# A Hyena-style block with a gated MLP on one core: queueing the first vector steps of each convolution behind the stage ahead, and moving the norm's small steps

## The chip, the core and the metric

The kernel runs on one core of a Trainium2 chip. The core has engines with a queue of instructions each: TensorE (PE) for matrix products, VectorE (DVE) and ScalarE (ACT) for elementwise work, GpSimd (POOL), and SyncE (SP), which issues the transfers here. [...]The time is that of one execution on the device in microseconds (us); before the change it is 519.38 us, the median of three runs (519.25 to 520.62). Inputs and weights are bf16.

## The reference, cut to what matters

There are 2048 rows of 576 values. A first half mixes along the rows (a shift convolution of four taps, a gate, a long convolution with a filter as long as the sequence), a second half is a gated MLP with 4608 hidden values. Both sit behind a layer norm with scales from a condition vector.

```python
h  = layernorm(x) * (1 + ca) + sa
# long convolution over the rows, written with FFTs in the reference
kv = shift4(k, shift_k) * v
y  = causal_conv(kv, ssm_k) + kv * ssm_D
x  = x + ga * (h * y)
h  = layernorm(x) * (1 + cb) + sb
x  = x + gb * ((silu(h @ w1) * (h @ w3)) @ w2)
```

## The kernel before

The rows are cut into 8 blocks of 256 (numbered `s`), two to a row block of 512 (`r` = 0 to 3). The long convolution is done block by block: the spectrum `X` of a block of `kv` and the spectrum `V` of a block of the filter (from two neighbouring pieces `W`) come from small matmuls with a Fourier basis; VectorE multiplies pairs of them and adds the products into `z`; small matmuls turn `z` back (`inverse`). The MLP of row block `r` runs on TensorE (`stream`: up and gate, then `down`), and while it runs the convolution of the two blocks of row block `r+1` is done beside it. That convolution is a Python generator: each `yield` says how many microseconds of VectorE work were recorded, and the MLP loop takes steps from it at a set rate (`advance`). The order in which the steps are recorded isn't yet that in the queues: a scheduler places each engine's instructions when the program is built, and puts a later recorded one ahead if it takes it to be ready and the engine to be free. `behind(engine)` keeps what is recorded under it behind the last instruction recorded for that engine so far.

```python
def behind(self, engine):
    last = [i for i in self.nc.cur_bb.bb.instructions if i.engine == engine.engine][-1]
    return self.tc.issue_after(last)

def kv_rows(self, s):                      # shift convolution and gate, 8 VectorE steps
    nc.vector.tensor_mul(kv[:], kh[:, 3:5, :], tap(0))
    yield 0.75
    for j in (1, 2, 3):
        nc.vector.tensor_mul(tmp[:], kh[:, 3 - j:5 - j, :], tap(j))
        nc.vector.tensor_add(kv[:], kv[:], tmp[:])
        yield 1.5
    nc.vector.tensor_mul(kv[:], kv[:], vt[:])
    ...

def v_block(self, s):                      # V from W(s) and W(s-1), 4 VectorE steps
    ...
        nc.vector.tensor_add(V[:, 0:6:3, :], W[:, 0:4:2, :], Wp[:, 1:4:2, :])
        nc.vector.tensor_sub(V[:, 1:6:3, :], W[:, 1:4:2, :], Wp[:, 0:4:2, :])
    ...

def pair(self, X, V, s, last=False):       # z(s) gets X * V
    if s not in self.accs:
        self.accs[s] = self.acc.tile([P, 6, D], BF16, name=f"z{s % 2}", tag=f"z{s % 2}")
        nc.vector.tensor_mul(self.accs[s][:], X[:], V[:])
        yield 2.0
        return
    p = self.prod.tile([P, 6, D], BF16, name="p", tag="p")
    with self.behind(nc.vector) if last else nullcontext():
        nc.vector.tensor_mul(p[:], X[:], V[:])
    yield 2.0
    nc.vector.tensor_add(z[:], z[:], p[:])
    yield 2.0

def conv(self, s0):                        # the two blocks s0, s1 of the next row block
    def filters():
        yield from self.k_rows(s1)
        yield -4.0
        yield from self.v_block(s0)
        yield from self.w_spectrum(s1)
    def old():
        V, X = self.old_v(s0 - 1, s0), self.old_x(1, s0)
        yield from self.pair(X, V, s0)
        for j in range(2, s0):
            ...                            # pairs of earlier blocks, for s1 and s0
        yield from self.gate_stats(s0)
        yield from self.kv_rows(s0)
        self.gate_var(s0)
    yield from self.mix(filters(), old())
    ...
    yield from self.mix(self.x_spectrum(s0), beside())   # TensorE reads kv(s0) here
    yield from self.x_sums(s0)
    yield from self.pair(self.X[s0], V0, s0)
    ...                                    # outcome(s0): inverse, residual, second norm;
                                           # kv_rows(s1), x_spectrum(s1) beside it; outcome(s1)

def hide(k):                               # MLP: one pair of tiles out of PSUM
    nc.scalar.activation(h3, gus[k][:, 0, :], ACT.Silu)
    nc.scalar.copy(u[:], gus[k][:, 1, :])
    nc.vector.tensor_mul(h3, h3, u[:])
    self.advance(rate * 2.05)              # steps of the convolution are recorded here
```

The row statistics go over three engines: ScalarE sums (`ln_sums`), VectorE and then GpSimd make `1/sqrt(var)` (`ln_var`), VectorE makes the shift (`ln_shift`), ScalarE applies both (`gate_rows` for the first norm, `normed_act` for the second).

Of the kernel before, what the change touches and what calls it, by code (L numbers as in the profile page):

```python
# [44 lines left out]
class _Kernel:  # L45
# [275 lines left out]
        nc.vector.tensor_add(both, both, odd)  # L321
        yield 1.5

    def kv_rows(self, s):

        nc = self.nc
        kh, vt = self.kh, self.vt
        kv = self.kvp.tile([P, 2, D], BF16, name="kv", tag="kv")
        tmp = self.kvp.tile([P, 2, D], BF16, name="kvt", tag="kvt")

        def tap(j):
            a = self.shk[:, j, :]
            return bass.AP(tensor=a.tensor, offset=a.offset, ap=[list(a.ap[0]), [0, 2], [1, D]])
        nc.vector.tensor_mul(kv[:], kh[:, 3:5, :], tap(0))
        yield 0.75
        for j in (1, 2, 3):
            nc.vector.tensor_mul(tmp[:], kh[:, 3 - j:5 - j, :], tap(j))  # L337
            nc.vector.tensor_add(kv[:], kv[:], tmp[:])  # L338
            yield 1.5
        nc.vector.tensor_mul(kv[:], kv[:], vt[:])  # L340
        self.kv = kv
        yield 0.75
# [38 lines left out]
            odd = self.kvp.tile([P, 2, D], BF16, name="Wo", tag="Wo")  # L381
            yield from self.forward2(self.Fk, self.kT, W[:, 0:2, :], odd[:], W[:, 2:4, :])

    def v_block(self, s):

        nc = self.nc
        W = self.Wl[s]
        V = self.spec.tile([P, 6, D], BF16, name="V", tag="V")
        if s == 0:
            nc.vector.tensor_copy(V[:, 0:6:3, :], W[:, 0:4:2, :])  # L390
            VS = W[:, 1:4:2, :]
        else:
            Wp = self.Wl[s - 1]
            nc.vector.tensor_add(V[:, 0:6:3, :], W[:, 0:4:2, :], Wp[:, 1:4:2, :])
            nc.vector.tensor_sub(V[:, 1:6:3, :], W[:, 1:4:2, :], Wp[:, 0:4:2, :])
            VS = V[:, 1:6:3, :]
        nc.vector.tensor_add(V[:, 2:6:3, :], V[:, 0:6:3, :], VS)
        yield 2.25
        nc.vector.tensor_sub(V[:, 1:6:3, :], VS, V[:, 0:6:3, :])
        self.V[s] = V  # L400
        yield 0.75

    def pair(self, X, V, s, last=False):

        nc = self.nc
        if s not in self.accs:
            self.accs[s] = self.acc.tile([P, 6, D], BF16, name=f"z{s % 2}", tag=f"z{s % 2}")
            nc.vector.tensor_mul(self.accs[s][:], X[:], V[:])  # L408
            yield 2.0
            return  # L410
        z = self.accs[s]
        p = self.prod.tile([P, 6, D], BF16, name="p", tag="p")
        with self.behind(nc.vector) if last else nullcontext():
            nc.vector.tensor_mul(p[:], X[:], V[:])  # L414
        yield 2.0
        nc.vector.tensor_add(z[:], z[:], p[:])  # L416
        yield 2.0
# [58 lines left out]
    def center(self, dst, src, mean, rstd):  # L476
        self.nc.vector.tensor_scalar(dst, src, mean, rstd, op0=ALU.subtract, op1=ALU.mult)

    def behind(self, engine):

        last = [i for i in self.nc.cur_bb.bb.instructions if i.engine == engine.engine][-1]
        return self.tc.issue_after(last)
# [10 lines left out]
    def gate_var(self, s):  # L493
        self.l1[s] = self.ln_var(*self.l1[s])

    def gate_rows(self, s):

        x1 = self.xo[s]
        r, b = self.ln_shift(*self.l1.pop(s))
        hg = self.lnp.tile([P, 2, D], BF16, name="hg", tag="hg")  # L500
        with self.behind(self.nc.scalar):
            for i in range(2):
                self.nc.scalar.activation(hg[:, i, :], x1[:, i, :], ACT.Identity, bias=b[:, i:i + 1],
                                          scale=r[:, i:i + 1])
        self.hg[s] = hg
# [56 lines left out]
        self.center(row[:, cc, 0:D], x1[:, cc, :], m, r)  # L562
        self.center(row[:, cc, D:640], x1[:, cc, 512:D], m, r)

    def normed_act(self, s, r, b):
        row, x1 = self.h2row, self.xo[s]
        for cc in range(2):
            for lo, hi, at in ((0, D, 0), (512, D, D)):
                self.nc.scalar.activation(row[:, cc, at:at + hi - lo], x1[:, cc, lo:hi], ACT.Identity,  # L569
                                          bias=b[:, cc:cc + 1], scale=r[:, cc:cc + 1])  # L570
# [168 lines left out]
    def outcome(self, s, fill, waits, between=None, quick=False):  # L739


        def steps():
            nc = self.nc
            yield self.real_parts(s)
            yield -waits[0]
            y = self.lnp.tile([P, 2, D], BF16, name="y", tag="y")
            for cc in range(2):
                nc.scalar.copy(y[:, cc, :].rearrange("p (h d) -> p h d", h=2), self.inverse(s, cc)[:, :, 0:H])
            yield -waits[1]
            self.residual(s, y)  # L750
            yield 1.5
            if between is not None:
                between()
            if quick:
                st = []
                for cc in range(2):
                    st.append(self.quick_stats(self.xo[s][:, cc, :], "l2"))
                    yield 1.25
                for cc in range(2):
                    self.normed(s, cc, *st[cc])  # L760
                    yield 0.75
            else:
                sums = [self.small.tile([P, 2], F32, name="l2" + k, tag=t) for k, t in (("s", "ssum"), ("q", "ssq"))]
                for i in range(2):
                    with self.behind(nc.scalar):
                        self.ln_sums(self.xo[s], i, *sums)
                    yield 0.0
                yield -waits[2] / 2
                stats = self.ln_var(*sums, "l2")
                yield -waits[2] / 2  # L770
                r, b = self.ln_shift(*stats)
                with self.behind(nc.scalar):
                    self.normed_act(s, r, b)
            yield -waits[3]
            self.accs.pop(s)
            self.hg.pop(s)
        yield from self.mix(steps(), fill)

    def turn_all(self, s):
# [6 lines left out]
    def conv_second(self):  # L786
        yield from self.gate_stats(1)
        yield from self.kv_rows(1)
        block = self.v_block(1)
        with self.behind(self.nc.vector):  # L790
            cost = next(block)
        yield cost

        def beside():
            yield from block
            self.gate_var(1)
            yield from self.pair(self.X[0], self.V[1], 1)
        yield from self.mix(self.x_spectrum(1), beside())
        self.mod_piece(5)
        self.gate_rows(1)  # L800
        yield from self.gate(1)
        self.load_k(2)
        yield from self.x_sums(1)
        yield from self.pair(self.X[1], self.V[0], 1)
        yield from self.outcome(1, self.mix(self.filter_ahead(2)), (5.0, 3.5, 0.0, 2.0), quick=True)
        self.turn_all(1)
        yield 0.0

    def conv(self, s0):
        s1 = s0 + 1  # L810
# [6 lines left out]
        def filters():  # L817
            yield from self.k_rows(s1)
            yield -4.0
            yield from self.v_block(s0)  # L820
            yield from self.w_spectrum(s1)

        def old():
            V, X = self.old_v(s0 - 1, s0), self.old_x(1, s0)
            yield from self.pair(X, V, s0)
            for j in range(2, s0):
                X = self.old_x(j, s0)
                yield from self.pair(X, V, s1)
                V = self.old_v(s0 - j, s0)
                yield from self.pair(X, V, s0)  # L830
            self.V1 = V
            yield from self.gate_stats(s0)
            yield from self.kv_rows(s0)
            self.gate_var(s0)
            if s0 == 2:
                yield from self.pair(self.X[0], self.V[s0], s0)
        yield from self.mix(filters(), old())
        X0, V0 = self.old_x(0, s0), self.old_v(0, s0)

        def beside():  # L840
            yield from self.v_block(s1)
            with self.behind(self.nc.sync):
                self.load_kv(s1)
            yield from self.gate_stats(s1)
            if s0 > 2:
                yield from self.pair(X0, self.V[s0], s0)
            self.X1 = self.old_x(1, s0)
            yield from self.pair(X0, self.V[s1], s1)
            self.gate_var(s1)
            self.gate_rows(s0)  # L850
            yield from self.gate(s0)
        yield from self.mix(self.x_spectrum(s0), beside())
        yield from self.x_sums(s0)
# [2 lines left out]
        def more():  # L856
            yield from self.pair(self.X1, self.V[s0], s1, True)
            yield from self.pair(self.X[s0], self.V1, s1)

        def others():  # L860
            yield from self.kv_rows(s1)
            yield from self.mix(self.x_spectrum(s1), more())
            yield from self.x_sums(s1)
        yield from self.outcome(s0, others(), (5.0, 4.5, 6.0, 0.0), lambda: self.gate_rows(s1))
# [317 lines left out]
```

## Time and profile before

| from the page of the profile | |
|---|---|
| span of the profiled execution | 516.6 us |
| PE busy | 495.2 us (96%) |
| DVE busy | 344.5 us (67%), 557 instructions |
| ACT busy | 293.6 us (57%) |
| POOL busy | 31.3 us (6%) |
| DMA | 107.80 MB, 209 GB/s |
| PEclk, all 40 slices | 9 tenths or more |

The page has the busy time of each engine, the span in 40 slices, and the chain of work that ended last. It calls a line of the kernel "L956" and an instruction by what it writes and reads. A matmul's end is modelled, so a busy PE isn't PE at its peak. By the first and last matmuls of lines 934, 945, 1046 and 1001, the MLP of r = 0 runs from about 34.5 us to 169.5 us, that of r = 1 to 290.6 us, that of r = 2 to 407 us, and that of r = 3 to the end. In r = 3 no convolution is left to do.

### The profile page before, as it was taken

Reading aid. Unit: us, or ns where it says so; the run is one execution under the profiler, and the core shown is the slowest. Engines: PE = TensorE matmul, PEld = TensorE weight load, DVE = VectorE, ACT = ScalarE, POOL = GpSimd, SP = SyncE. Lnnn points to the kernel's source line nnn. Section 1 sums busy time; section 2 is a strip of 40 time slices with the busy share of each in tenths; the row PEclk is TensorE's granted clock in tenths of the full one; section 3 lists DMA queues with packets and bytes.
Section 4 is the critical chain, followed back from the end, with each engine's and each line's share of the span. In section 5 each row is a group of like instructions: output and inputs, shape, how many; then the busy total and the mean of one; then the engine's idle time right before and its main releaser. Section 6 shows DMA issues by size and latency. Waiting matters only on the chain.

```text
span 516.6 us, 9251 instructions
## 1 busy us (share of the span) xinstructions
PE 495.2 (96%) x3650; PEld 293.5 (57%) x3650; DVE 344.5 (67%) x557; ACT 293.6 (57%) x581; POOL 31.3 (6%) x75
## 2 busy tenths in 40 slices
PE   7899899989899999999998999999999999999997
PEld 3567665456688444344676643444578644444775
DVE  8888899999997354979999626988972222222012
ACT  7658589657543468769443464886815355555000
POOL 3100000002000000000101000020000000000000
PEclk9999999999999999999999999999999999999999
DMA  8957949686979866558997559854555545532462
GB/s 271 301 173 217 313 157 299 194 256 212 293 236 355 264 211 196 177 164 275 333 318 203 161 151 349 315 201 124 174 139 140 159 123 164 173 111 76 117 182 69
DMA packets 102207, 107.80 MB, mean 209 GB/s; under 512 B 5075, under 2 KB 94228, under 8 KB 102164
## 3 DMA queue, kind: packets, MB, share of 16 engines
q1 hardware_dynamic: 102142, 107.21, 67.3%
q8 instruction: 28, 0.46, 0.4%
q14 instruction: 15, 0.12, 0.1%
q10 hardware_dynamic: 22, 0.01, 0.0%
HBM read 96.00 MB, written 11.21 MB: 208 GB/s over the span
## 4 chain that ended last, share of the span: by engine, by line
PE 66%; DVE 21%; ACT 5%; DMA 3%; issue 3%; POOL 2%; SPq 0%; DVEq 0%; POOLq 0%; ACTq 0%
PE ps L934 24%; PE ps L1046 21%; PE ps L1001 12%; DVE p L414 4%; PE ps L945 4%; DVE z L416 3%; DVE z L408 2%; DVE h L956 2%; DMA kh<-in_A_k_dram 2%; PE ps L316 2%; POOL l2r L454 1%; DVE kv L338 1%; DVE kvt L337 1%; ACT junk L446 1%; DMA wst<-in_B_w_dram 1%
## 5 line engine op out<-in xcount | busy, mean ns | idle before, releaser
L934 PE MATMUL ps<-h2T,wst 128*128 128x512 bf16 (+1 forms) x1056 | 200.6, 341 | 1.1 <-ACT W L318 0.8
L934 PEld LDWEIGHTS <-wst 128*128 128x128 bf16 x1056 | 100.2, 98 | 85.7 <-issue 13.8
L1046 PE MATMUL ps<-wst,h 128*128 128x288 bf16 x1152 | 145.0, 286 | 3.9 <-ACT u L955 2.0
L1046 PEld LDWEIGHTS <-h 128*128 128x128 bf16 x1152 | 112.2, 98 | 33.3 <-issue 4.8
L953 ACT ACTIVATE h<-ps 128x512 bf16<-128x512 f32 x108 | 64.8, 600 | 67.6 <-PE ps L945 42.1
L1001 PE MATMUL ps<-h2T,wst 64*128 64x512 bf16 x648 | 70.3, 377 | 0.2 <-DMA wst<-in_B_w_dram 0.2
L956 DVE TENSOR_TENSOR h<-h,u 128x512 bf16<-128x512 bf16 x108 | 45.0, 421 | 36.3 <-ACT u L955 36.2
L955 ACT CAST u<-ps 128x512 bf16<-128x512 f32 x108 | 63.4, 587 | 0.0
L414 DVE TENSOR_TENSOR p<-X,V 128x3456 bf16<-128x3456 bf16 x28 | 54.7, 1954 | 4.2 <-DMA V<-Vd 2.2
L416 DVE TENSOR_TENSOR z<-z,p 128x3456 bf16<-128x3456 bf16 x28 | 54.7, 1954 | 0.2
L1001 PEld LDWEIGHTS <-wst 64*128 64x128 bf16 x648 | 31.5, 94 | 38.7 <-DMA wst<-in_B_w_dram 0.7
L1016 DVE TENSOR_TENSOR h<-h,u 128x512 bf16<-128x512 bf16 x36 | 15.3, 426 | 55.3 <-ACT u L1015 55.3
L1013 ACT ACTIVATE h<-ps 128x512 bf16<-128x512 f32 x36 | 21.5, 598 | 36.5 <-PE ps L1001 36.5
L1063 DVE TENSOR_TENSOR og<-ps,gbrow 128x288 bf16<-128x288 f32 x32 | 13.2, 451 | 41.1 <-PE ps L1046 41.1
L446 ACT ACTIVATE junk<-x 128x576 bf16<-128x576 bf16 x54 | 37.2, 689 | 0.5
L945 PE MATMUL ps<-h2T,wst 64*128 64x512 bf16 (+1 forms) x264 | 33.0, 342 | 0.0
L604 ACT ACTIVATE h2T<-ps,sbcol,cbcol 128x256 bf16<-128x256 bf16 x35 | 16.7, 569 | 19.4 <-PE ps L574 19.4
L569 ACT ACTIVATE h2row<-x,l2n,l2r 128x576 bf16<-128x576 bf16 (+1 forms) x24 | 13.7, 643 | 19.4 <-DVE l2n L460 19.4
L454 POOL TENSOR_TENSOR l2r<-l2v,neghalf 128x2 f32<-128x2 f32 x6 | 11.2, 1868 | 181.2 <-DVE l2v L453 181.2
L337 DVE TENSOR_TENSOR kvt<-kh,shk 128x1152 bf16<-128x1152 bf16 x24 | 18.1, 754 | 4.3 <-DMA kh<-in_A_k_dram 4.2
L1015 ACT CAST u<-ps 128x512 bf16<-128x512 f32 x36 | 20.9, 581 | 0.0
L945 PEld LDWEIGHTS <-wst 64*128 64x128 bf16 x264 | 8.5, 94 | 21.0 <-issue 20.8
(140 smaller groups left out, 398.6 us busy)
## 6 DMA issues: line engine op xcount, KB each, us to landing
wst<-in_B_w_dram SPq DMA_DIRECT2D x80, 512.0 KB, 5.0
wst<-in_B_w_dram SPq DMA_DIRECT2D x72, 288.0 KB, 3.4
X<-Xd SPq DMA_DIRECT2D x8, 864.0 KB, 6.7
Xd<-X SPq DMA_DIRECT2D x6, 864.0 KB, 6.0
wst<-in_B_w_dram SPq DMA_DIRECT2D x80, 64.0 KB, 3.3
kh<-in_A_k_dram SPq DMA_DIRECT2D x7, 720.0 KB, 7.3
Vd<-V SPq DMA_DIRECT2D x4, 864.0 KB
V<-Vd SPq DMA_DIRECT2D x4, 864.0 KB, 9.6
```

Of the source, the lines that this page charges most:

```text
L337: nc.vector.tensor_mul(tmp[:], kh[:, 3 - j:5 - j, :], tap(j))
L414: nc.vector.tensor_mul(p[:], X[:], V[:])
L416: nc.vector.tensor_add(z[:], z[:], p[:])
L446: self.nc.scalar.activation(junk[:], src[:, i, :], func, scale=scale, accum_out=out[:, col:col + 1])
L934: nc.tensor.matmul(gus[k][:, i, a * n:(a + 1) * n], w[:, 5 * i + ct, (fi + a) * P:(fi + a + 1) * P], hT[:, ct, t0:t1], start=(first and ct ...
L945: nc.tensor.matmul(gus[k][:, i, a * n:(a + 1) * n], w[rows, 4, (fi + a) * P:(fi + a + 1) * P], hT[rows, 4, t0:t1], start=(first and a == 0 ...
L953: nc.scalar.activation(h3, gus[k][:, 0, :].rearrange("p (a t) -> p a t", a=m), ACT.Silu)
L955: nc.scalar.copy(u[:], gus[k][:, 1, :])
L956: nc.vector.tensor_mul(h3, h3, u[:].rearrange("p (a t) -> p a t", a=m))
L1001: nc.tensor.matmul(gus[f][:, i, :], w[rows, 5 * i + ct if ct < 4 else 4, cols], hT[rows, ct, :], start=swap == 0 and ct == 0, stop=swap == ...
L1013: nc.scalar.activation(h3, gus[f][:, 0, :], ACT.Silu)
L1046: nc.tensor.matmul(acc[t], self.h3[:, f0 + f, t * P:(t + 1) * P], w[:, f, :], start=(f0 + f == 0), stop=(f0 + f == NF - 1))
```

## The change

The convolution's first VectorE steps are to stay behind the stage ahead of them, so that the scheduler can't put them between steps that the stage ahead still waits for. The first product of a `z`, the first step and the three tap products of `kv_rows(s0)`, and the first two steps of `v_block(s0)` are now recorded under `behind(nc.vector)`. Apart from that, the last small step of each norm (`ln_shift`) gets a place of its own: `gate_shift` is recorded some steps after `gate_var` and ahead of `gate_rows`, and in the second norm a gap is left between `ln_shift` and the rows, which are recorded one row group at a time.

```diff
-    def kv_rows(self, s):
+    def kv_rows(self, s, last=False):
...
-        nc.vector.tensor_mul(kv[:], kh[:, 3:5, :], tap(0))
+        with self.placed(last):
+            nc.vector.tensor_mul(kv[:], kh[:, 3:5, :], tap(0))
         yield 0.75
         for j in (1, 2, 3):
-            nc.vector.tensor_mul(tmp[:], kh[:, 3 - j:5 - j, :], tap(j))
+            with self.placed(last):
+                nc.vector.tensor_mul(tmp[:], kh[:, 3 - j:5 - j, :], tap(j))
...
-    def v_block(self, s):
+    def v_block(self, s, last=False):
...
+            with self.placed(last):
+                nc.vector.tensor_add(V[:, 0:6:3, :], W[:, 0:4:2, :], Wp[:, 1:4:2, :])
+                nc.vector.tensor_sub(V[:, 1:6:3, :], W[:, 1:4:2, :], Wp[:, 0:4:2, :])
...                                            # pair: both first products
+            with self.placed(last):
+                nc.vector.tensor_mul(self.accs[s][:], X[:], V[:])
...
+    def placed(self, last):
+        return self.behind(self.nc.vector) if last else nullcontext()
...
+    def gate_shift(self, s):
+        self.l1[s] = self.ln_shift(*self.l1[s])
...
-        r, b = self.ln_shift(*self.l1.pop(s))
+        r, b = self.l1.pop(s)
...                                            # second norm
-                r, b = self.ln_shift(*stats)
-                with self.behind(nc.scalar):
-                    self.normed_act(s, r, b)
+                scales = self.ln_shift(*stats)
+                yield -3.0
+                for cc in range(2):
+                    self.normed_act(s, cc, *scales)
+                    yield -1.0
...                                            # conv
-            yield from self.v_block(s0)
+            yield from self.v_block(s0, True)
...
-            yield from self.pair(X, V, s0)
+            yield from self.pair(X, V, s0, True)
...
-            yield from self.kv_rows(s0)
+            yield from self.kv_rows(s0, True)
...
         def beside():
             yield from self.v_block(s1)
+            self.gate_shift(s0)
...
+            self.gate_rows(s0)
             yield from self.pair(X0, self.V[s1], s1)
             self.gate_var(s1)
-            self.gate_rows(s0)
...
         def others():
             yield from self.kv_rows(s1)
+            self.gate_shift(s1)
```

More of the change, by code (lines that the diff above doesn't have):

```diff
@@ L393, in v_block @@
             Wp = self.Wl[s - 1]
-            nc.vector.tensor_add(V[:, 0:6:3, :], W[:, 0:4:2, :], Wp[:, 1:4:2, :])
-            nc.vector.tensor_sub(V[:, 1:6:3, :], W[:, 1:4:2, :], Wp[:, 0:4:2, :])
+            with self.placed(last):
+                nc.vector.tensor_add(V[:, 0:6:3, :], W[:, 0:4:2, :], Wp[:, 1:4:2, :])
+                nc.vector.tensor_sub(V[:, 1:6:3, :], W[:, 1:4:2, :], Wp[:, 0:4:2, :])
             VS = V[:, 1:6:3, :]
@@ L407, in pair @@
             self.accs[s] = self.acc.tile([P, 6, D], BF16, name=f"z{s % 2}", tag=f"z{s % 2}")
-            nc.vector.tensor_mul(self.accs[s][:], X[:], V[:])
+            with self.placed(last):
+                nc.vector.tensor_mul(self.accs[s][:], X[:], V[:])
             yield 2.0
@@ L412, in pair @@
         p = self.prod.tile([P, 6, D], BF16, name="p", tag="p")
-        with self.behind(nc.vector) if last else nullcontext():
+        with self.placed(last):
             nc.vector.tensor_mul(p[:], X[:], V[:])
@@ L563, in normed, with normed_act @@
         self.center(row[:, cc, D:640], x1[:, cc, 512:D], m, r)
-    def normed_act(self, s, r, b):
+    def normed_act(self, s, cc, r, b):
         row, x1 = self.h2row, self.xo[s]
-        for cc in range(2):
+        with self.behind(self.nc.scalar):
             for lo, hi, at in ((0, D, 0), (512, D, D)):
@@ L788, in conv_second @@
         yield from self.kv_rows(1)
[L789 to L792, printed above, removed]
+        block = self.v_block(1, True)
+        yield next(block)
         def beside():
@@ L797, in beside @@
             yield from self.pair(self.X[0], self.V[1], 1)
+            self.gate_shift(1)
         yield from self.mix(self.x_spectrum(1), beside())
```

## The prediction

> **What bounds the kernel now.** I read the slices first, then TensorE's waits, then the timelines of PE and DVE around the longest waits. The slices say that PE hardly pauses.
>
> ```profile
> PE   7899899989899999999998999999999999999997
> DVE  8888899999997354979999626988972222222012
> PEclk9999999999999999999999999999999999999999
> ```
>
> PE is busy 495.2 of 516.6 us. Listing its pauses over 0.25 us in the timeline gives 14.6 us in all, so nothing that only removes waits can bring 3%. DVE is full from about 60 to 145 us (first half of r = 0's MLP and beyond), less so in r = 1 and 2. The longest pauses that this change could touch:
>
> ```profile
> PE ps L542 <- DVE z L528: 2.6, 1, 2.6
> PE ps L1046 <- ACT u L955: 2.0, 2, 1.5
> PE ps L542 <- DVE z L524: 1.9, 1, 1.9
> PE ps L1046 <- DVE og L1063: 1.9, 1, 1.9
> PE ps L367 <- ACT u L955: 0.9, 1, 0.9
> ```
>
> The third of them is what the change aims at. In the DVE timeline the next stage's first product (L408) stands between two steps of the inverse that TensorE waits for:
>
> ```profile
> 54.41 0.75 DVE L522 TENSOR_TENSOR z<-z 128x1152 bf16<-128x1152 bf16 x1
> 55.07 1.95 DVE L408 TENSOR_TENSOR z<-X,V 128x3456 bf16<-128x3456 bf16 x1
> 56.94 0.75 DVE L524 TENSOR_TENSOR z<-z 128x1152 bf16<-128x1152 bf16 x1
> ```
>
> But running ahead also fills holes. From 65.88 us DVE does `kv` for block 2 in time it had free; PE reads that `kv` (L316) much later:
>
> ```profile
> 65.88 0.76 DVE L334 TENSOR_TENSOR kv<-kh,shk 128x1152 bf16<-128x1152 bf16 x1
> 67.21 0.42 DVE L956 TENSOR_TENSOR h<-h,u 128x512 bf16<-128x512 bf16 x1
> 67.55 0.75 DVE L338 TENSOR_TENSOR kv<-kv,kvt 128x1152 bf16<-128x1152 bf16 x1
> 70.14 0.75 DVE L320 TENSOR_TENSOR W<-W,Wo 128x1152 bf16<-128x1152 bf16 x1
> 70.81 0.75 DVE L337 TENSOR_TENSOR kvt<-kh,shk 128x1152 bf16<-128x1152 bf16 x1
> 74.49 0.75 DVE L340 TENSOR_TENSOR kv<-kv,vt 128x1152 bf16<-128x1152 bf16 x1
> ```
>
> ```profile
> 79.39 0.41 PE L316 MATMUL ps<-kv,Fb 128*128 128x288 bf16 x2 [0.39 <-ACT u L955]
> ```
>
> In the next two row blocks the lead is larger. `kv` of block 4 is finished at 160.2 us and read first at 199.89; that of block 6 is read first at 331.40. So the stretches 146 to 170 us and 262 to 290 us, when PE works on `down`, carry the next block's convolution:
>
> ```profile
> 146.00:170.00 24.00, 24.00 (x208) 19.23 (x206) 18.17 (x26) 10.05 (x22) 0.69 (x1) 1.00 0.90 292
> 173.00:204.00 31.00, 31.00 (x157) 12.73 (x156) 15.02 (x29) 21.84 (x44) 0.69 (x1) 1.00 0.71 221
> 294.00:331.00 37.00, 37.00 (x185) 14.94 (x185) 21.37 (x28) 23.99 (x47) 0.00 (x0) 1.00 0.79 270
> ```
>
> (Columns: length; busy PE, PE loads, DVE, ACT, POOL; clock; DMA.) DVE is busy 18.2 of 24 us in the first, and only half of the time in the other two.
>
> [...]the granted clock is 1.00 throughout; this matters below.
>
> **The change part by part.** No instruction is added or removed: 559 on DVE before and after. It is order alone, so I set the order of each engine's instructions in the two built programs side by side and walked DVE's new order with durations from the old trace. Start to start in a full queue: 1.87 us for a 3456-wide step (55.07 to 56.94), 0.67 for a 1152-wide one (70.14 to 70.81), 0.34 for L956 (67.21 to 67.55).
>
> *r = 0.* L408 leaves the inverse of block 1, so PE's 1.87 us pause goes, and all up to the norm rows comes 1.87 earlier. Then DVE has nothing allowed but four L956 and two W steps; the last of these L956 waits for a tile that ACT released at 72.64, now 70.8, so L408 starts at about 71.2. From there to the end of `kv` the new order has 3 wide steps (5.6), 14 of 1152 (9.4), 2 L956 (0.7) and small ones (0.2): 15.9 us, so `kv` is ready at about 87.1 instead of 75.2. The W copies on ACT wait for V's second step, now 75.1 (74.6 before); PE resumes there at about 76.6, as before, which eats the 1.87. The scheduler moved only 16 matmuls ahead of L316, so PE asks at about 81.0 and waits **6.1 us**. From then on it is 6.0 behind the old trace. The inverse of block 2 still waits about 2 us for L528 (the shift taps of block 3 now also wait for `kh`, 7.3 us from issue to landing), and `kv` of block 3 costs perhaps 0.9. At the start of `down`, L367 now stands 48 matmuls into it, so its 1.55 us pause should go. Sum: 5.9 + 0.9 - 1.55 = **+5.3**.
>
> *r = 1.* Nearly nothing of blocks 4 and 5 stands in `down` any more. The convolution starts after r = 1's first L956, which ended 4.4 us after its first matmul (173.9 against 169.5). To the end of `kv` for block 4: 10 wide steps (18.7), 18 of 1152 (12.1), 13 L956 (4.4), small ones (0.2): 35.4 us, ready 39.8 us after the start. PE asks after 140 MLP matmuls in both programs, 199.89 - 169.52 = 30.4 us after the start. Wait **9.4 us**. Saved: the 0.93 at L367 (48 matmuls later now), 0.43 at L529 and 1.87 at `og`, since DVE is free when `og` comes. Sum: 9.4 - 3.2 = **+6.2**.
>
> *r = 2.* Start to first L956 3.8 us; then 16 wide steps (29.9), 18 of 1152 (12.1), 19 L956 (6.5), small ones (0.2): 48.7, ready at 52.5 us. PE asks at 331.40 - 290.63 = 40.8, plus 8 matmuls moved ahead (1.6): 42.4. Wait **10.1**, less 0.48 at the start of `down`: **+9.6**.
>
> *The norm's small steps.* `l1n` and `l2n` no longer hold DVE while POOL works (5.2 and 4.1 us of DVE idle time in all, 0.6 to 0.9 each). In r = 0, where DVE is full, this is worth about 1.6 us and is in the walk; elsewhere it lies beside other work.
>
> Together +21.1 us: 519.4 + 21.1 = 540.5. To that comes the clock. [...]I count less than half of it, since nothing here has shown it. Prediction: **542 us**.
>
> **The rivals.** (a) *The aim is met*: the waits for L524, L528, `og` and u go and nothing comes back, 519.4 - 1.9 - 2.6 - 1.9 - 2.5 = 510.5 us. For it speaks that these waits are really in the trace and that L408 really stands in the way. Against it, the half-idle stretches above: in r = 1 `kv` has a lead of 40 us today because it is done in `down`, and the new order forbids that. (b) *A wash*: the lost lead is absorbed because DVE is half idle from 173 to 204 us. That idle time is about 16 us, and in r = 0 some of the displacement is made up; if my sums were 10% too high the waits in r = 1 and 2 would shrink by 3.5 and 5, and with the gains the total would be near 531. To come to zero they would have to be 25% too high. (c) *Worse*: [...]Loads of old X and V wait for DVE to free a buffer, and weight loads stand behind them; with DVE 10 us late PE may wait for `wst` as well, and the clock may drop each time. That would give 550 to 556.
>
> **Range and chances.** The walk's durations are measured and PE's need for `kv` is a data dependence, so I hold slower to be nearly certain; the size hangs on 16 and 10 wide steps being counted right and on the clock. Range 527 to 556, low end from (b), high end from (c). Faster by over 2% 0.03, within 2% 0.12, slower by over 2% 0.85.
>
> **What would show it.** Among PE's waits a new group "L316 <- DVE kv" of three long ones, 6, 9 and 10 us; DVE nearly idle late in each `down`; `og`, L524 and L367 gone from the waits; PEclk under 9 in the slices of the long waits if the clock drops. I am wrong if no L316 waits over 3 us, or if DVE runs the convolution's steps faster than in the old trace.

## The result and the profile after

The changed kernel takes **548.15 us** (median; 547.61 to 548.30) against 519.58 us for the kernel before (519.25 to 520.62) beside it. The ratio is 1.054, with a 95% interval of 1.053 to 1.056: 28.6 us slower. The span of the profiled execution went from 516.6 to 546.2 us.

The slices first, the same three rows as before:

```profile
PE   7999986989999992999999999479999999999997
DVE  8889688898451898597832599979973121222011
PEclk9999987999999996999999999979999999999999
```

PE now has three holes (slices 7, 16, and 26 to 27), and behind each the granted clock falls under nine tenths. DVE's row shows the other side: slices 11 to 13 were nine, nine and seven and are now four, five and one, and at the holes it has seven to nine.

PE's waits name the holes (us in total, times, longest; two waits ahead of r = 0, of 3.0 and 1.0 us, are left out):

```profile
PE ps L316 <- DVE kv L342: 26.4, 4, 10.6
PE ps L947 <- ACT W L318: 1.9, 1, 1.9
PE ps L1059 <- ACT u L968: 0.9, 1, 0.9
```

L316, which reads `kv`, waited for nothing of note before. The waits for the inverse's `z` (2.6 and 1.9 us) and for `og` (1.9) are gone. In the timeline of PE the waits for `kv` are 5.14 us in r = 0, 9.79 in r = 1 and 10.60 in r = 2, and a small one of 0.85. Leaving out the wait ahead of the first matmul, PE's pauses over 0.1 us are 35.1 us, where they were 14.5. (The prediction's 14.6 us hold these, and not only those over 0.25 us, which are 13.3 us before and 33.7 after.)

The first aim is met. In DVE's timeline the inverse's steps stand together, with no product between them:

```profile
54.57 0.75 DVE L532 TENSOR_TENSOR z<-z 128x1152 bf16<-128x1152 bf16 x1
55.35 0.76 DVE L534 TENSOR_TENSOR z<-z 128x1152 bf16<-128x1152 bf16 x1
```

But that product (now L412) and all that is placed behind it come later, `kv` last:

```profile
71.43 1.95 DVE L412 TENSOR_TENSOR z<-X,V 128x3456 bf16<-128x3456 bf16 x1
73.30 0.75 DVE L335 TENSOR_TENSOR kv<-kh,shk 128x1152 bf16<-128x1152 bf16 x1
...
86.66 0.75 DVE L342 TENSOR_TENSOR kv<-kv,vt 128x1152 bf16<-128x1152 bf16 x1
```

```profile
87.55 1.12 PE L316 MATMUL ps<-kv,Fb 128*128 128x288 bf16 x4 [5.14 <-DVE kv L342]
```

Before, that last step began at 74.49 us, so `kv` is 12.2 us later and PE is waiting for it. The stretches that answer to the three of before (the first two at the same distance from the end of r = 0's `down`, the third 0.9 us nearer to the end of r = 1's):

```profile
153.00:177.00 24.00, 24.00 (x206) 19.19 (x205) 7.08 (x21) 10.69 (x23) 0.69 (x1) 1.00 0.93 301
180.00:211.00 31.00, 26.83 (x132) 10.81 (x133) 30.93 (x38) 19.79 (x39) 2.02 (x1) 0.98 0.69 212
308.00:345.00 37.00, 36.75 (x188) 15.34 (x192) 36.02 (x37) 24.03 (x48) 0.00 (x0) 1.00 0.88 308
```

In `down` DVE's busy time (the third figure after the length) fell from 18.2 to 7.1 us; in the next two row blocks it rose from 15.0 to 30.9 and from 21.4 to 36.0 us. Half-idle DVE time in r = 1 and 2 was filled, and it was not enough.

Two losses make up the span: PE's pauses, +20.6 us, and PE's busy time, 495.2 to 503.3 us, **+8.1 us** for the same work (the remaining 0.9 us is smaller gaps). The windows around the waits show where the second comes from (the column after POOL is the granted clock):

```profile
73.10:76.50 3.40, 0.89 (x8) 0.48 (x6) 3.40 (x8) 3.40 (x10) 0.17 (x1) 0.99 0.94 264
76.50:79.90 3.40, 3.40 (x16) 2.15 (x15) 3.40 (x4) 1.51 (x3) 1.04 (x1) 0.51 0.32 94
...
86.70:93.50 6.80, 5.73 (x17) 1.98 (x19) 6.41 (x10) 1.99 (x4) 0.00 (x0) 0.50 0.89 285
...
209.60:219.80 10.20, 3.02 (x9) 1.18 (x10) 7.12 (x10) 0.64 (x1) 4.30 (x1) 0.50 0.32 101
...
352.90:363.20 10.30, 4.36 (x12) 1.61 (x12) 9.62 (x12) 2.63 (x6) 2.72 (x1) 0.50 0.53 183
```

PE is busy for 3.40 + 5.73 + 3.02 + 4.36 = 16.5 us at half clock. From 76.49 us, at clock 0.51, 16 products of L947 (128x256) took 3.53 us; from 80.49, at full clock, 16 took 1.92. Half of the 16.5 us, 8.3 us, is an estimate of what PE would have saved at full clock; 8.1 us is the measured rise.

By the ends of the four `down` stages (last matmul), the row blocks' lengths:

| us | r = 0 | r = 1 | r = 2 | r = 3 |
|---|---|---|---|---|
| before | 169.7 | 121.1 | 116.2 | 105.8 |
| after | 176.8 | 129.0 | 130.5 | 106.2 |
| difference | +7.1 | +7.8 | +14.3 | +0.4 |

### The profile page after: what moved, and what is told of

Its sections match the earlier page's. It is cut to its first block, busy times and chain, and to the rows that moved or that the text cites. A ratio compares the mean times of both kernels' runs of the same rounds, so it can differ in the third digit from the quotient of the medians.

```text
span 546.2 us, 9253 instructions
## 1 busy us (share of the span) xinstructions
PE 503.3 (92%) x3630; PEld 295.8 (54%) x3650; DVE 344.5 (63%) x557; ACT 294.5 (54%) x581; POOL 29.6 (5%) x75
## 4 chain that ended last, share of the span: by engine, by line
PE 55%; DVE 29%; ACT 7%; DMA 4%; issue 2%; POOL 2%; SPq 0%; POOLq 0%; ACTq 0%; DVEq 0%
PE ps L1059 22%; PE ps L947 14%; PE ps L1014 12%; DVE z L420 6%; DVE p L418 6%; DMA wst<-in_B_w_dram 3%; DVE h L969 3%; PE ps L958 2%; ACT junk L450 2%; POOL l1r L458 2%; PE ps L316 2%; DVE z L412 1%; DVE kvt L339 1%; DVE kv L340 1%; PE ps L552 1%
## 5 line engine op out<-in xcount | busy, mean ns | idle before, releaser
L947 PE MATMUL ps<-h2T,wst 128*128 128x512 bf16 (+1 forms) x1037 | 205.2, 347 | 3.5 <-ACT W L318 1.9
L947 PEld LDWEIGHTS <-wst 128*128 128x128 bf16 x1056 | 102.2, 100 | 91.7 <-issue 21.4
L1014 PE MATMUL ps<-h2T,wst 64*128 64x512 bf16 x648 | 70.5, 376 | 0.4 <-DMA wst<-in_B_w_dram 0.4
L968 ACT CAST u<-ps 128x512 bf16<-128x512 f32 x108 | 63.2, 585 | 0.0
L969 DVE TENSOR_TENSOR h<-h,u 128x512 bf16<-128x512 bf16 x108 | 45.2, 421 | 18.8 <-ACT u L968 18.7
L1014 PEld LDWEIGHTS <-wst 64*128 64x128 bf16 x648 | 31.2, 94 | 39.4 <-DMA wst<-in_B_w_dram 1.7
L316 PE MATMUL ps<-kv,Fb 128*128 128x288 bf16 x48 | 10.4, 318 | 26.4 <-DVE kv L342 26.4
L318 ACT CAST X<-ps 128x576 bf16<-128x576 f32 x24 | 15.0, 644 | 24.6 <-PE ps L316 24.6
L614 ACT ACTIVATE h2T<-ps,sbcol,cbcol 128x256 bf16<-128x256 bf16 x35 | 16.8, 570 | 14.5 <-PE ps L584 14.5
L412 DVE TENSOR_TENSOR z<-X,V 128x3456 bf16<-128x3456 bf16 x7 | 13.7, 1955 | 16.4 <-PE ps L552 16.2
L458 POOL TENSOR_TENSOR l1r<-l1v,neghalf 128x2 f32<-128x2 f32 (+1 forms) x8 | 13.0, 1628 | 174.7 <-DVE l1v L457 174.7
L316 PEld LDWEIGHTS <-Fb 128*128 128x128 bf16 x48 | 4.0, 102 | 33.6 <-issue 27.6
```

Source lines behind the costliest of these rows:

```text
L316: nc.tensor.matmul(ps[:, h, 0:H], basis[:, cc, cs], rhs[:, cc, h * H:(h + 1) * H], start=True, stop=True)
L458: self.nc.gpsimd.tensor_tensor(rstd[:], var[:], self.neghalf[:, 0:n], op=ALU.pow)
L947: nc.tensor.matmul(gus[k][:, i, a * n:(a + 1) * n], w[:, 5 * i + ct, (fi + a) * P:(fi + a + 1) * P], hT[:, ct, t0:t1], start=(first and ct ...
L969: nc.vector.tensor_mul(h3, h3, u[:].rearrange("p (a t) -> p a t", a=m))
L1014: nc.tensor.matmul(gus[f][:, i, :], w[rows, 5 * i + ct if ct < 4 else 4, cols], hT[rows, ct, :], start=swap == 0 and ct == 0, stop=swap == ...
```

## The experiments

The theory to be tested: the new order lets `kv` of a row block's first block come too late for L316, and the clock falls in those waits. `kv` is recorded last of all the convolution's steps ahead of L316; placed, it stays there, and the scheduler may no longer pull it forward into `down`. Rivals: that the other placed steps (first product, V) or the norm steps are the cost, that PE merely asks too soon, and that the clock is no cost of its own. Each run was timed beside the kernel before, which was at 519.4 to 519.6 us.

### The norm steps alone

```diff
 after, with no step of kv_rows(s0), v_block(s0) and the first product under placed(); gate_shift,
 the gap and the split normed_act stay
```

> Only the moved norm steps; the three placements are left out. Theory (the lost lead of kv is the whole cost): kv is as early as in the kernel before, so no wait of L316 for kv and a full clock; the scheduler now also puts the transposes of the filter (knat) 48 matmuls into down, so the pauses of 1.55 and 0.93 us there go: about 517 us. Rival (the later norm steps cost part of the loss): 525 us or more, with waits for hg or h2row.

Measured: 523.05 us (521.91 to 524.39), ratio 1.007 (1.005 to 1.009). It lies between the two figures, so both were missed: moving the norm's small steps costs about 3.5 us. The pauses at the start of `down` (1.55 and 0.93 us) went, but the wait at the inverse of block 2 is 2.9 us (2.6 before) with one of 0.7 behind it, and the clock is halved for 3.4 us after them (mean 0.996); PE waits for `og` appear in `down` of r = 0 (1.8 us) and at the start of r = 1 (1.1).

### The placing alone

```diff
 after, with ln_shift, gate_rows and normed_act where the kernel before has them
```

> Only the three placements; the norm steps as before. Theory: all of the loss is here and the norm part even saved the two pauses at the start of down, so about 550 us, with three waits of L316 for kv of 5, 10 and 10 us and the clock halved after each. Rival (norm steps cost part): clearly under the 548.2 of the full change, 535 to 543 us.

Measured: 543.53 us (542.78 to 545.03), ratio 1.046 (1.045 to 1.048). The time lies 0.5 us over the rival's range and 6.5 us under the theory's 550. The three waits for `kv` are all there (5.2, 9.1 and 9.9 us), and PE is busy 501.0 us. So placing is +23.9 of the +28.6; with the 3.5 of the norm steps alone the two halves of the change nearly add up (27.4).

### Placing kv alone

```diff
-            yield from self.kv_rows(s0)
+            yield from self.kv_rows(s0, True)
 and nothing else (before)
```

> Only kv_rows(s0) placed, first products and v_block free. Theory: what counts is the work that DVE has between the first MLP product of a row block and the end of kv. It falls from 35.4 to 17.5 us in r = 1 and from 48.6 to 31.1 us in r = 2, so kv is ready at 22 and 35 us where PE asks at 30 and 42: no wait there; in r = 0 it is 15.4 instead of 18.6 us, a wait of 2 to 3 us: 520 to 524 us. Rival (any placing of kv costs its own 9 to 10 us per row block): 540 us or more.

Measured: 534.52 us (533.44 to 538.78), ratio 1.031 (1.026 to 1.036). The size lay between the two figures. The group of waits is the same, with 1.9, 4.2 and 9.9 us:

```profile
PE ps L316 <- DVE kv L342: 16.1, 3, 9.9
```

I had counted only the vector work ahead of `kv`. In the timeline `kv`'s steps also stand behind MLP products recorded with them (L961 here), which DVE can start no sooner than ACT brings `u`. From 171 to 186 us, in r = 1, DVE does seven such products and nothing else: it is busy 2.9 of 15 us, waits 1.6 to 2.2 us for `u` ahead of each, and starts `kv` only at 195.83. So here the place in the queue set the time, more than the amount of work.

### The first product alone

```diff
-            yield from self.pair(X, V, s0)
+            yield from self.pair(X, V, s0, True)
 and the first step of z in pair() under placed(last), nothing else (before)
```

> Only the first product of z placed. Theory: kv stays 12 and 14 us ahead of the first MLP product in r = 1 and 2, so no wait for kv; the 1.87 us pause before L524 goes, and some of it may come back at the W copies: 517 to 519.5 us. Rival (the first products are what the rest queues behind): 530 us or more.

Measured: **516.2 us** (515.27 to 516.99), ratio 0.993 (0.992 to 0.995), faster than the kernel before and 0.8 us below the range expected. PE's waits for L524 and `og` are gone, and L1046's for `u` fell from 2.0 to 0.5 us. One got longer, from 2.6 to 3.5 us:

```profile
PE ps L549 <- DVE z L535: 3.5, 1, 3.5
```

and the window behind it (104.0 to 107.2 us) is at clock 0.50.

### The waits filled with useless products

```diff
+        with self.behind(self.nc.tensor):
+            self.warm({2: 22, 4: 44, 6: 44}[s0], self.shk[:, 0, 0:512])
         yield from self.mix(self.x_spectrum(s0), beside())
 (after)
```

> The kernel after the change, with products of shk by itself that nobody reads, recorded on TensorE just ahead of each block's first L316: 22, 44 and 44 of 128x512 (some 0.21 us each, so about 5, 9 and 9 us), which fill the three waits for kv with work of no use. Clock theory: kv still comes when it comes, so the start of L316 hardly moves, but TensorE doesn't pause and its clock stays full; the 6 to 8 us that the lower clock cost go, 540 to 542 us. Rival (the clock is no cost, the busy time grew for another reason): 548 us or more.

Measured: 549.16 us (548.49 to 550.99), ratio 1.058 (1.056 to 1.061). The size is the one that the rival gave, but not for its reason. The clock did stay up, mean 0.994 in place of 0.972. In r = 1 the fill took up the wait to the last 0.3 us:

```profile
204.98 9.66 PE L639 MATMUL ps<-shk,ident 128*128 128x512 bf16 x44
214.94 0.40 PE L316 MATMUL ps<-kv,Fb 128*128 128x288 bf16 x2 [0.30 <-DVE kv L342]
```

PE's busy time less the fill (522.5 - 4.9 - 9.7 - 9.7 = 498.2 us) is 5.1 below that of the change, so the lower clock really costs PE time. But the end didn't come sooner. PE waited 4.3 us for weights, which hardly happened in the change (0.4 us at L1014):

```profile
PE ps L1061 <- DMA wst<-in_B_w_dram: 3.1, 3, 1.1
...
PE ps L1016 <- DMA wst<-in_B_w_dram: 1.2, 1, 1.2
```

and in r = 2 PE came to the fill 40.6 us after the row block's start, where it had come to L316 after 42.5, so that a wait of 4.4 us for `kv` came on top of 9.7 us of fill. Removing a loss at the clock thus doesn't return it one to one here.

### Asking for kv later

```diff
+        yield {2: 6.0, 4: 10.5, 6: 12.0}[s0]
         yield from self.mix(self.x_spectrum(s0), beside())
 (after)
```

> The kernel after the change, with one line added: ahead of the x_spectrum of the first block of each row block, 6, 10.5 and 12 us of further steps pass, so that TensorE gets 44, 52 and 48 MLP products more ahead of L316 than before. Theory (the loss is TensorE asking before kv is ready, and the clock that this takes along): the waits for kv shrink under 1.5 us each, the clock stays full, 520 to 528 us. Rival (VectorE's later start costs the time wherever TensorE asks: the same waits come back at the inverse, at h2T or at the end of down): 540 us or more.

Measured: 544.14 us (542.89 to 545.57), ratio 1.048 (1.046 to 1.050). The rival's outcome: 4 of the 28.6 us came back. PE's waits for `kv` went from 26.4 to 5.1 us, and others took their place (first five waits but for the start of the kernel):

```profile
PE ps L1060 <- DMA wst<-in_B_w_dram: 5.2, 4, 2.9
PE ps L316 <- DVE kv L342: 5.1, 3, 2.2
PE ps L584 <- ACT h2row L579: 4.7, 4, 1.8
PE ps L948 <- DMA wst<-in_B_w_dram: 2.9, 2, 1.9
```

The clock fell here too, to a mean of 0.977: in the 3.4 us from 117.5, 223.3 and 359.9 us it was 0.55, 0.55 and 0.54. By row blocks the difference to the kernel before is +6.8, +2.8, +9.3 and +6.8 us. The last is new: the tail of r = 2's convolution now ends in r = 3, which waits for its `h2row`. So it isn't only that PE asks too soon. The vector work starts too late, and `h2row`, at the end of that work, is waited for in its stead. What made the weights late (8.1 us of waits for `wst` in all) isn't shown.

### The first product alone, and an earlier start

```diff
-FIRST_DUE = 12.0
+FIRST_DUE = 9.0
 (on the kernel with the first product alone)
```

> The kernel before, with only the first product of z placed (as in the run that did that alone, 516.2 us), and the convolution of the first row block started 3 us earlier (FIRST_DUE 9 in place of 12). If what that run still lost is its 3.5 us wait at the inverse of block 2 and the halved clock behind it, and this comes from VectorE being late there: 512 to 515 us, that wait under 2 us. If VectorE is full there whatever it starts with: 516 us again.

Measured: **514.20 us** (513.51 to 514.84), ratio 0.990 (0.988 to 0.992), as expected and the best of all. The wait at the inverse of block 2 is 0.7 us, one for `kv` of block 3 is 1.15, and PE's pauses over 0.1 us sum to 8.1 us. Behind these two the clock is still halved once, for 3.4 us (mean 0.997).

### The first product alone, and one product behind the inverse

```diff
-                yield from self.pair(X0, self.V[s1], s1)      (in beside, for s0 == 2)
+                yield from self.pair(X0, self.V[s1], s1)      (in more)
 (on the kernel with the first product alone)
```

> As the run with only the first product of z placed (516.2 us), with the product of X(0) and V(3) and its sum recorded behind the inverse of block 2 in place of ahead of it. Takes about 3.7 us of VectorE work out of the way of that inverse: if this is what its 3.5 us wait is made of, the wait falls under 1 us, the clock stays full, 511 to 514 us. Otherwise 516 us.

Measured: 517.81 us (516.83 to 518.81), ratio 0.997 (0.996 to 0.998). A miss: that wait stays at 3.0 us, `kv` of block 3 adds 1.35, and the clock falls behind both (mean 0.992). It wasn't that product that held the inverse.

### The change without placing kv

```diff
-            yield from self.kv_rows(s0, True)
+            yield from self.kv_rows(s0)
 (after, one argument)
```

> The kernel after the change with one part undone: the steps of kv_rows(s0) are recorded freely again. In the built order kv of block 4 and of block 6 are then done ahead of the first L956-like product of their row block, with 12 and 16 us of VectorE work to spare. Theory (placing these four steps is what turns the rest into a loss, since it forces kv behind all that was recorded ahead of it): no wait of L316 over 1 us in r = 1 and 2, clock full but for one stretch in r = 0, about 520 us (the 516.2 of the first product alone and the 3.5 of the norm steps). Rival (placing kv is worth only the +15 us that it cost alone): 533 us.

Measured: 524.76 us (522.51 to 526.14), ratio 1.010 (1.006 to 1.013). One argument brings back **23.4 of the 28.6 us**. `kv` of block 4 is done at 142.5 us and read at 202.1, that of block 6 at 254.2 and read without a wait:

```profile
329.92 0.42 PE L316 MATMUL ps<-kv,Fb 128*128 128x288 bf16 x2
```

The 524.8 us is over the 520 that I expected. In the profiled execution r = 2 is 8.9 us longer than before (r = 0 1.9 longer, r = 1 3.3 shorter). PE waits 3.3 and 1.9 us for the `z` of block 6's inverse, with the clock halved behind it (mean 0.990). A step of `kv` of block 7 stands between steps of that inverse:

```profile
356.96 0.75 DVE L342 TENSOR_TENSOR kv<-kv,vt 128x1152 bf16<-128x1152 bf16 x1
...
357.97 0.75 DVE L538 TENSOR_TENSOR z<-z 128x1152 bf16<-128x1152 bf16 x1
```

But so it did before, where PE didn't wait there:

```profile
353.47 0.76 DVE L338 TENSOR_TENSOR kv<-kv,kvt 128x1152 bf16<-128x1152 bf16 x1
354.14 0.76 DVE L528 TENSOR_TENSOR z<-z 128x1152 bf16<-128x1152 bf16 x1
```

So that step isn't what is new. The first vector step of that inverse came later, 66.3 us after the row block's start against 61.0 before, while PE came to it 66.2 us after the start in both. What delayed it by these 5.3 us isn't shown.

### The first product and the norm steps

```diff
-            yield from self.v_block(s0, True)
+            yield from self.v_block(s0)
 (on the run before this one)
```

> As the run before, with the two steps of v_block freed too: only the first product of z is placed, and the norm steps are moved. If the parts add: 516.2 + 3.5, about 519.7 us. If the norm steps' cost came from the order that the first product mends (the wait for z at the inverse of block 2 and the clock behind it): 515 to 517 us.

Measured: 519.23 us (517.70 to 521.29), ratio 1.000 (0.999 to 1.001). The parts add: the first product's gain pays for the norm steps. Placing V on top of these two costs 5.5 us.

### The V steps alone

```diff
-            yield from self.v_block(s0)
+            yield from self.v_block(s0, True)
 and nothing else (before)
```

> The kernel before with only the two steps of v_block placed. By the built order kv keeps its lead (8.5 and 6.9 us of work ahead of the row block's first product): 518 to 521 us, no wait for kv. If placing V costs by itself what the placed parts lost beyond kv alone (543.5 - 534.5 = 9 us): 528 us.

Measured: 518.05 us (516.65 to 521.49), ratio 0.998 (0.996 to 0.999). By itself placing V costs nothing.

### The earlier start alone

> The kernel before with nothing but the convolution of the first row block started 3 us earlier (FIRST_DUE 9). If the 514.2 us of the run with both is the sum of two independent gains (3.2 by the first product, 2.0 by the start), this is 517.4 us. If the earlier start pays only once the product is out of the inverse's way: 519 us or more.

The edit is that of the earlier start above, on the kernel before. Measured: 517.97 us (517.18 to 519.30), ratio 0.997 (0.996 to 0.998). Two independent gains: 3.4 us for the product and 1.5 for the start make 514.5, and 514.2 was measured.

### What the parts come to

| placed, moved | us | against before |
|---|---|---|
| first product | 516.20 | -3.4 |
| V | 518.05 | -1.4 |
| norm steps | 523.05 | +3.5 |
| kv | 534.52 | +14.9 |
| first product, norm steps | 519.23 | -0.2 |
| first product, V, norm steps | 524.76 | +5.3 |
| first product, V, kv | 543.53 | +23.9 |
| all | 548.15 | +28.6 |

The single parts add up to 13.6 us, less than half of the whole. `kv` is worth 14.9 us alone and 23.4 on top of the others. A likely reason is that what it stands behind has then itself been pushed back: in the built order 35 us of vector work lie between r = 1's first L969 and the end of `kv` of block 4, against 17.5 with `kv` placed alone, and the waits for `kv` are 5.1, 9.8 and 10.6 us against 1.9, 4.2 and 9.9. Which of the other parts does this wasn't tried.

## Why the prediction was right, and where it wasn't

**The mechanism and the three waits** held. Predicted were 6.1, 9.4 and 10.1 us, measured 5.1, 9.8 and 10.6. L412 started at 71.43 us (predicted 71.2), `kv` of block 2 was ready at 87.4 (87.1), `kv` of block 4 came 40.0 us after the start of r = 1 (39.8), that of block 6 53.1 after the start of r = 2 (52.5). Walking the new order with durations from the old trace gave each of these four times within 0.6 us. (The page counts 557 instructions on DVE on both sides, not 559.) The wait in r = 0 was 1.0 us shorter than predicted because PE asked at 82.4 us and not at 81.0: it did the matmuls ahead of that at half clock. PE's added pauses were put at 21.1 us and were 20.6, and that the sums agree so well is partly luck: by row blocks they were +1.6, +6.7 and +12.1 us where 5.3, 6.2 and 9.6 were predicted.

**The clock** is the term that was mis-sized. I counted 1.5 us for it (542 less the sum of 540.5), my estimate, which nothing in the trace of before had shown; it took 8.1. I had only the three long waits in mind. The trace has four halved stretches of 3.4, 6.8, 10.2 and 10.2 us, the first behind two pauses of 0.56 and 1.95 us that I hadn't counted. With 8.1 in place of 1.5 the sum would have been 548.6 us; that this is so near the 548.15 measured rests on the same luck. How it would be without it isn't settled by that: filling the waits gave PE 5.1 us back and the kernel none.

**r = 0** came out near the sum (+7.1 against +5.3) for a partly other reason. "The inverse of block 2 still waits about 2 us" was wrong: only 0.73 and 0.69 us were waited there, for ACT. PE's pauses in r = 0 thus grew by only 1.6 us (10.6 to 12.2), and the halved clock, 3.4 + 5.7 us of work at half rate, cost about 4.6 more by the same estimate; 0.9 us stay unassigned.

**r = 1** was +7.8 against +6.2. The `og` and L367 waits went, as the sum has it; the wait was 0.4 us longer, and most of the rest is the clock (3.0 us of work at half rate, an estimate of 1.5 us; PE's busy time in this row block rose by 0.8).

**r = 2** was +14.3 against +9.6: the wait 0.5 us longer, the clock 2.2 (an estimate, from 4.4 us of work at half rate), a wait for `u` of 0.95 and one for `h2row` of 0.53 that I didn't have. These make 4.2 of the 4.7.

**The norm's small steps** failed in sign: "this is worth about 1.6 us" in r = 0, and elsewhere lay beside other work. Alone they cost 3.5 us, and on top of the first product 3.0. A DVE that doesn't sit idle for POOL isn't a gain where the steps brought forward in its stead push back what PE waits for; which steps these are I haven't separated by a run.

**The rivals.** *The aim is met* was true of the waits it named, but for 0.95 us for `u`, and of one part: the first product alone, which is all the inverse of block 1 needed, gained 3.4 us. *A wash* had DVE's idle time take up the lead; DVE is indeed full now in r = 1 (30.9 of 31 us), and the waits were still 9.8 and 10.6. *Worse* had the size (550 to 556) nearest, by the clock and the loads together. In the trace of before, loads of old X and V (L439) do wait for DVE to free a buffer, 3.1 us in all for the product at L414. In the change itself the loads did nothing (0.4 us of waits for `wst`); they came forward in the fill (4.3 us) and in the later ask (8.1 us).

## What to carry to other kernels

A step that a scheduler has pulled into another stage's slack may be what keeps TensorE fed: before fixing its place, look up when its reader asks, and pin only the step that stands in the way (here one product: 516.2 us, 514.2 with an earlier start) and not the one whose reader comes next. Parts pinned behind each other in one queue don't add up; take back single parts from the whole as well as trying them alone. A new wait of TensorE is to be booked with what it does to the clock (here 8.1 us of busy time on top of 20.6 us of pauses).

## What the runs showed of the hardware

In the change's trace the granted clock was 0.50 in four stretches. They begin at 76.42, 86.67, 209.54 and 352.90 us and last 3.41, 6.83, 10.24 and 10.24 us. Ahead of them PE paused, but in two cases not all of the time: of the 3.41 us ahead of each it was busy for 0.97, 0.00, 0.81 and 0.00 us. In the run that asks later, of the 3.40 us up to 117.5, 223.3 and 359.9 us PE was busy for 1.30, 1.49 and 1.15 us, and the clock in the 3.40 us behind was 0.55, 0.55 and 0.54.

A pause of one length didn't always have the same effect. The kernel before and the kernel with the earlier start alone have the same pause of 1.87 us, for the `z` of L524. In the first it ends at 57.75 us and the clock stays full:

```profile
53.30:56.72 3.42, 2.42 (x20) 1.70 (x19) 3.42 (x5) 2.63 (x4) 0.00 (x0) 1.00 0.73 199
56.72:60.13 3.41, 2.38 (x21) 1.96 (x21) 1.69 (x5) 1.35 (x3) 0.00 (x0) 1.00 1.11 337
```

In the second it ends at 57.54 us, and from 58.30 us PE is at half clock:

```profile
54.89:58.30 3.41, 1.43 (x11) 1.01 (x12) 3.27 (x5) 1.39 (x4) 0.00 (x0) 1.00 0.82 237
58.30:61.71 3.41, 3.41 (x18) 2.28 (x16) 1.09 (x2) 1.74 (x3) 0.00 (x0) 0.50 1.06 366
```

The twelve products of L542 behind the pause took 1.63 us in the first and 2.34 us in the second. The pause of 2.58 us at 102.8 in the kernel before dropped nothing either: from 101.09 to 107.92 us the clock is 1.00. What decides between these cases isn't shown; no run was made to find it.
